# Moving the gate's rows and most second-layer weights to GpSimd's queue, the gate ahead of the weights, and query rows behind the contexts

## The chip, the cores and the metric

The kernel runs on one core of a Trainium2 chip. The metric is device time in microseconds (us), lower is better; a time is the median of several executions. The engines are named as in the profile: PE (TensorE matmul), PEld (its weight load), DVE (VectorE), ACT (ScalarE), POOL (GpSimd) and SP (SyncE). SP and POOL here do almost nothing but issue DMA transfers, each in the order of its own instruction stream.

## The reference

Two branches read the same input `x` (2048 rows of 512) and are mixed row by row with a gate. Branch A is attention with 32 query heads of 16 dimensions over one shared key and value head; branch B is a two-layer network with a squared ReLU. All is float32.

```
g = sigmoid((x * gate_w).sum(-1))                 # one number a row
q, k, v = x @ wq, x @ wk, x @ wv                  # 32 heads of 16; one head of 16; one of 16
a = softmax(q k^T / 4) v, heads joined, @ wo
h = relu(x @ w1 + b1) ** 2                        # 512 -> 1792
b = h @ w2 + b2                                   # 1792 -> 512
out = g * a + (1 - g) * b
```

## The kernel before, in words

The whole program is unrolled and its order is written out by hand: a Python planner follows modelled times of PE, DVE and ACT (`at_pe`, `at_dve`, `at_act`) and puts each instruction where its engine should be free. Waits are then added for every dependency, so an engine stands still where the model was too early.

**Attention.** The 2048 query rows are four chunks `c` of 512; each chunk has eight groups of four heads, so there are 32 groups `it`. A group is cut into 32 units of work `u`: 16 key tiles of 128, times two halves `q` of 256 rows. For each unit PE writes the scores (line 881), ACT (or DVE's copy at line 902, then ACT) makes the exponentials (line 918), and PE adds the context into an accumulator (line 938). `phase` writes scores for a block of 6 to 9 units, mixed with matmuls of another "unit" of dense work (a span), then `context` writes the contexts of the block. Scores run `AHEAD = 4` units before the contexts. Where a half is finished, `finish` (line 974) lets ACT copy the accumulator into a tile `accs`, of which there is one, and after the second half SP issues two transfers out of it: `oc` (line 999) and `lq` (line 1000).

**Query rows.** A dense unit of the query stage (`q_unit`, 15 of them in the loop, each a span) makes 128 query columns for one chunk, splits them in a high and a low part, and writes both to DRAM with `q_write`: `qs<-qr` from SP and `qs<-ql` from POOL (line 372); after each fourth one `qnorm` writes norms (`qs<-nrm`, line 436). `q_load` (line 445) fetches the rows of one group from there into one of two `qa` tiles, with eight SP transfers (line 450), each of which waits until the scores of the group before last are done.

**Gate.** `gates()` queues chores for DVE: `gate_load(i)` fetches two rows of tiles of `x` (512 KB) into one of two buffers, `stage` and `rows` (line 662), the first time also the gate's weights `gwb` (line 660); `gate_sum(i)` (line 670) multiplies and sums one of 16 tiles. A load goes out after the sums that used its buffer; its sums are held in the plan for `3 * LANDS` = 18 us. `gate_exps` and `gate` finish `g` and `1 - g`.

**Weights of the dense network.** `w_load(half)` fetches tile `n` of the first (`half` 0) or second (`half` 1) layer, 256 KB each, 14 a layer, into a staging place (`wf`, or half of a stage buffer; tile `n` uses the place of tile `n - 2`), by SP at line 491. `w_round` rounds it (ACT line 535 or DVE line 519) once `w_ready` says that more than `2 * LANDS` = 12 us of modelled PE time have gone by since the load; `w_rest` (line 528) takes the remainder, and asks for the next load, which is written at the end of the span. `w_keep` stores the split tiles to DRAM from POOL (line 514) for the later chunks. `room = [3, 4]` bounds how many split tiles there may be before the dense network begins, which is after the query stage.

**Order of DVE's extra work.** `soon` is a list of (span, cost, call): an entry is called at the latest at the start of that span, and earlier if DVE has time. `spend` fills DVE's gaps: first remainders of weights, then `soon`, divisions, roundings, biases, and then `chores` in their order, each with its modelled cost.

## Time and profile before

| | |
|---|---|
| median of 3 runs | 1183.03 us (1180.05 to 1184.37) |
| the profiled execution | 1185.62 us, of which the span from first to last instruction is 1183.7 us |
| PE, PEld, DVE, ACT, POOL busy | 1170.7, 783.6, 687.5, 1023.1, 72.1 us |
| DMA on SP's queue (q1) and on POOL's (q0) | 90.40 MB and 37.45 MB |

Rows of a timeline give start, duration, engine, line, operation, output and inputs, and in brackets the idle time of the engine just before and what ended it. The query stage, with the gate and the first weights beside it, takes about the first 150 us of the span; the rest is attention with the dense network and the output projection in between.

### The profile page before, as it was taken

What the parts mean: (1) busy time and instruction counts of PE and PEld (TensorE: products, weight loads), DVE (VectorE), ACT (ScalarE), POOL (GpSimd) and SP (SyncE); (2) the same over time, 40 slices, a digit from 0 to 9 for tenths busy, and PEclk for the clock granted to TensorE, in tenths of its full rate; (3) what the DMA queues carried; (4) which work ended last, traced back from release to release, by engine and by line L of the source; (5) the groups of instructions that cost most, each with busy time, mean ns of one, the idle gap of its engine ahead of it and who ended that gap; (6) DMA issues with size and microseconds to landing.
All of it is one profiled execution on the core that took longest, in us unless ns stands there. A gap on an engine that the chain in (4) does not pass through costs nothing.

```text
span 1183.7 us, 32009 instructions
## 1 busy us (share of the span) xinstructions
PE 1170.7 (99%) x13807; PEld 783.6 (66%) x13807; DVE 687.5 (58%) x1154; ACT 1023.1 (86%) x1133; POOL 72.1 (6%) x129
## 2 busy tenths in 40 slices
PE   9998999999999999999999999999999999999997
PEld 4665666676666666666666666666666666666664
DVE  6885777774764744463566636535556537544554
ACT  7796889998988888888888888888889889888884
POOL 1010101010100000100000000000000000001000
PEclk9998999999999999999999999999999999999999
DMA  7456444342253423230333404324214224322101
GB/s 255 128 155 170 116 145 171 101 161 105 98 178 119 163 71 104 96 99 29 117 135 113 136 6 143 128 65 153 64 47 154 90 65 131 109 72 79 56 37 38
DMA packets 53735, 130.25 MB, mean 110 GB/s; under 512 B 14218, under 2 KB 14714, under 8 KB 53080
## 3 DMA queue, kind: packets, MB, share of 16 engines
q1 hardware_dynamic: 38568, 90.40, 24.2%
q0 software_dynamic: 14736, 37.45, 9.6%
q8 instruction: 109, 1.79, 0.6%
q10 hardware_dynamic: 288, 0.33, 0.1%
q14 instruction: 34, 0.28, 0.1%
HBM read 87.91 MB, written 35.64 MB: 104 GB/s over the span
## 4 chain that ended last, share of the span: by engine, by line
PE 96%; DMA 2%; SPq 1%; ACT 1%; DVE 1%; issue 0%; DVEq 0%; ACTq 0%
PE acc L938 38%; PE mm L1245 32%; PE s L881 18%; PE x L881 5%; DMA stage<-in_xs 1%; SPq L450 1%; DMA oc<-accs 1%; ACT e L918 0%; PE acc L571 0%; PE mm L211 0%; PE mm L313 0%; DVE e L902 0%; DVE ot L1205 0%; PE s L322 0%; PE acc L358 0%
## 5 line engine op out<-in xcount | busy, mean ns | idle before, releaser
L918 ACT ACTIVATE e<-s 128x1024 f32<-128x1024 f32 x765 | 748.6, 1024 | 109.4 <-PE s L881 106.6
L902 DVE COPY e<-x 128x512 f32<-128x512 f32 x518 | 358.3, 692 | 450.5 <-PE x L881 295.2
L938 PE MATMUL acc<-e,v_ext 128*32 128x256 f32 x8192 | 470.2, 381 | 0.0
L881 PE MATMUL s<-qa,k_aug 49*128 49x512 f32 x1530 | 408.2, 411 | 1.4 <-ACT e L918 1.3
L938 PEld LDWEIGHTS acc<-e,v_ext 128*32 128x32 f32 x8192 | 252.3, 110 | 193.3 <-issue 40.8
L918 ACT ACTIVATE e<-e 128x1024 f32<-128x1024 f32 x259 | 272.9, 1056 | 0.9 <-DVE e L902 0.9
L881 PEld LDWEIGHTS s<-qa,k_aug 49*128 49x128 f32 x1530 | 214.6, 185 | 86.9 <-ACT e L918 41.3
L1245 PE MATMUL mm<-w2p,hr 64*128 64x512 f32 x1128 | 242.5, 392 | 0.0
L881 PE MATMUL x<-qa,k_aug 49*128 49x512 f32 x518 | 214.5, 414 | 3.7 <-DVE e L902 3.7
L1245 PEld LDWEIGHTS mm<-w2p,hr 64*128 64x128 f32 x1128 | 160.5, 186 | 18.5
L881 PEld LDWEIGHTS x<-qa,k_aug 49*128 49x128 f32 x518 | 95.5, 184 | 39.5 <-DVE e L902 21.7
L1245 PE MATMUL mm<-xragain,w1p 64*128 64x512 f32 x448 | 119.5, 392 | 0.0
L1245 PE MATMUL mm<-xr,w1p 64*128 64x512 f32 x448 | 114.9, 392 | 0.0
L1245 PEld LDWEIGHTS mm<-xragain,w1p 64*128 64x128 f32 x448 | 70.0, 186 | 6.4
L1245 PEld LDWEIGHTS mm<-xr,w1p 64*128 64x128 f32 x448 | 68.4, 186 | 6.0
L1245 PE MATMUL mm<-xlagain,w1p 64*128 64x512 f32 x224 | 69.5, 395 | 0.0
L1245 PE MATMUL mm<-xl,w1p 64*128 64x512 f32 x224 | 66.5, 393 | 0.0
L1245 PE MATMUL mm<-more 64*128 64x512 f32 x216 | 60.2, 393 | 0.0
L992 ACT ACTIVATE accs<-acc 128x256 f32<-128x256 f32 x60 | 23.1, 385 | 29.6 <-PE acc L938 25.8
L764 DVE TENSOR_SCALAR big<-mm,b1t 128x512 f32<-128x512 f32 x56 | 41.6, 742 | 0.0
L765 DVE TENSOR_TENSOR big<-big 128x512 f32<-128x512 f32 x56 | 38.8, 692 | 1.9
L1245 PEld LDWEIGHTS mm<-xlagain,w1p 64*128 64x128 f32 x224 | 35.6, 186 | 4.7
(188 smaller groups left out, 824.4 us busy)
## 6 DMA issues: line engine op xcount, KB each, us to landing
w1p<-w1kept SPq DMA_DIRECT2D x42, 512.0 KB
w2p<-w2kept SPq DMA_DIRECT2D x35, 512.0 KB
qa<-qs SPq DMA_DIRECT2D x186, 64.0 KB
w1kept<-w1p POOLq DMA_DIRECT2D x14, 512.0 KB, 4.2
w2kept<-w2p POOLq DMA_DIRECT2D x12, 512.0 KB, 5.6
qs<-qr SPq DMA_DIRECT2D x16, 256.0 KB
ress<-res POOLq DMA_DIRECT2D x4, 1024.0 KB, 4.6
qs<-ql POOLq DMA_DIRECT2D x15, 256.0 KB, 7.5
```

What stands on the lines that cost most here:

```text
L450: nc.sync.dma_start(q[64 * r + row:64 * r + row + b - a].bitcast(F32), qs[it, r, a:b])
L764: nc.vector.tensor_scalar(h[0], p, b1t[:, f:f + 1], 0.0, op0=OP.add, op1=OP.max)
L765: nc.vector.tensor_tensor(h[0], h[0], h[0], OP.mult)
L881: nc.tensor.matmul(dst.rearrange("p (a n) -> p a n", a=2), k_aug[rows, kt * 128:(kt + 1) * 128], qa[it][rows, :, q * HC:q * HC + HC], star ...
L902: nc.vector.tensor_copy(e_half(u)[:, 2 * r:2 * r + 2], x.rearrange("p (a n) -> p a n", a=2))
L918: nc.scalar.activation(e_half(u), src, AF.Exp, scale=SCALE)
L938: nc.tensor.matmul(accs[q][h * 32:(h + 1) * 32], v_ext[:, kt], es[u][:, h % 2 * 2 + h // 2], start=kt == 0 and it > 0, stop=kt == NK - 1, ...
L992: nc.scalar.activation(a[:, q * HC:q * HC + HC], acc, AF.Copy)
L1245: nc.tensor.matmul((self.before if r else self).bank, a[p], b[p], start=not r and i == 0, stop=r == 1 and i == len(self.terms[1]) - 1, ski ...
```

## The change

Four edits go together. `w_load` issues tiles 0 to 11 of both layers from POOL instead of SP, tiles 12 and 13 stay on SP. `gate_load` issues the gate's weights and rows from POOL. The first two pairs of weight loads leave `soon` and become chores behind the gate sums 8 and 10, and `gates()` is called at span 3 at the latest, not 5, with no loads ahead of it. In the main loop `context` comes ahead of `q_load`, so that the copies and transfers of finished sums are written before the query loads of that block. The bias rows `b2t`, 256 KB once, go from POOL to SP.

```diff
-                nc.sync.dma_start(wf[half][n], w12[n, :, half * 512:half * 512 + 512])
+                (nc.gpsimd if n < NF - 2 else nc.sync).dma_start(wf[half][n], w12[n, :, half * 512:half * 512 + 512])
...
-                (2, 0.0, lambda: (w_load(0), w_load(1))), (2, 0.7, lambda: (act(0.64), wq_round(0), wq_rest(0)))]
-        soon += [(5, 0.0, lambda: (w_load(0), w_load(1), gates()))]
+                (2, 0.7, lambda: (act(0.64), wq_round(0), wq_rest(0))), (3, 0.0, lambda: gates())]
...
-                nc.sync.dma_start(gwb, bass.AP(tensor=gw.tensor, offset=gw.offset, ap=[[0, 128], [1, D]]))
+                nc.gpsimd.dma_start(gwb, bass.AP(tensor=gw.tensor, offset=gw.offset, ap=[[0, 128], [1, D]]))
             if i < NS:
-                nc.sync.dma_start(gate_rows[i // 2 % 2], xs[i:i + 2].rearrange("t p d -> p t d"))
+                nc.gpsimd.dma_start(gate_rows[i // 2 % 2], xs[i:i + 2].rearrange("t p d -> p t d"))
...
+        def w_loads():
+            w_load(0)
+            w_load(1)
 
         def gates():
             chores.append((0.0, lambda: gate_load(0)))
...
                 chores.append((0.77, lambda i=i: gate_sum(i)))
+                if i in (NS - 8, NS - 6):
+                    chores.append((0.0, w_loads))
...
-                    nc.gpsimd.dma_start(b2t[0], bass.AP(tensor=b2.tensor, offset=b2.offset, ap=[[0, 128], [1, D]]))
+                    nc.sync.dma_start(b2t[0], bass.AP(tensor=b2.tensor, offset=b2.offset, ap=[[0, 128], [1, D]]))
...
             phase(slots, min(u + m + AHEAD, total) - scored, m)
+            context(range(u, u + m))
             it = (u + m - 1) // (2 * NK)
             if it not in begun_q and it + 1 < NC * NG:
                 begun_q.add(it)
                 q_load(it + 1)
-            context(range(u, u + m))
```

## The prediction

> **What bounds the kernel now.** I read the page first: is one engine the bound? Then the waits of that engine, then its timeline around each wait, and from there backwards to what came late.

> ```profile
> span 1183.7 us, 32009 instructions
> PE 1170.7 (99%) x13807; PEld 783.6 (66%) x13807; DVE 687.5 (58%) x1154; ACT 1023.1 (86%) x1133; POOL 72.1 (6%) x129
> ```

> TensorE (PE) is busy 99% of the span, so only time in which PE stands still, or runs slowly, can be won without removing matmuls, and this change removes none. The waits of PE, longest first (total, times, longest):

> ```profile
> PE x L881 <- DVE e L902: 3.7, 2, 3.4
> PE s L881 <- ACT e L918: 1.3, 1, 1.3
> ```

> Two waits matter, both in the query stage. To price them with what follows them I use the distance between the starts of successive context blocks (line 938) in PE's timeline:

> ```profile
> 85.72 2.80 PE L938 MATMUL acc<-e,v_ext 128*32 128x256 f32 x48
> 92.15 0.50 PE L881 MATMUL s<-qa,k_aug 49*128 49x512 f32 x2 [1.33 <-ACT e L918]
> 94.70 3.23 PE L938 MATMUL acc<-e,v_ext 128*32 128x256 f32 x56
> 102.48 3.23 PE L938 MATMUL acc<-e,v_ext 128*32 128x256 f32 x56
> 110.74 0.79 PE L881 MATMUL x<-qa,k_aug 49*128 49x512 f32 x1 [3.43 <-DVE e L902]
> 116.59 3.23 PE L938 MATMUL acc<-e,v_ext 128*32 128x256 f32 x56
> ...
> 124.38 2.80 PE L938 MATMUL acc<-e,v_ext 128*32 128x256 f32 x48
> 131.71 3.23 PE L938 MATMUL acc<-e,v_ext 128*32 128x256 f32 x56
> 139.47 3.23 PE L938 MATMUL acc<-e,v_ext 128*32 128x256 f32 x56
> ```

> Undisturbed, a block of 48 to the next takes 131.71 - 124.38 = 7.33 us, a block of 56 takes 139.47 - 131.71 = 7.76. The first wait's block took 94.70 - 85.72 = 8.98, that is 1.65 too long; the second's 116.59 - 102.48 = 14.11, that is 6.35 too long. The second costs nearly twice its 3.43 us of standstill, and the stretches of 4 us show why (the last three figures are the granted clock, the DMA share and GB/s):

> ```profile
> 108.00:112.00 4.00, 1.26 (x6) 1.07 (x8) 2.34 (x6) 0.35 (x1) 0.00 (x0) 0.71 0.69 211
> 112.00:116.00 4.00, 4.00 (x20) 3.10 (x20) 1.56 (x4) 2.06 (x3) 0.70 (x1) 0.50 0.39 131
> 116.00:120.00 4.00, 4.00 (x66) 1.87 (x62) 2.58 (x4) 2.90 (x3) 0.00 (x0) 0.93 0.48 81
> ```

> After the standstill the clock was granted at 0.50 until about 116.5. The shorter wait left it at full speed. Together 8.00 us are to be had here.

> What came late in each case stands in the rows of ACT and DVE, and in the chain of waits (start, length, piece):

> ```profile
> 90.80 0.38 ACT L992 ACTIVATE accs<-acc 128x256 f32<-128x256 f32 x1 [2.41 <-DMA oc<-accs]
> 109.38 0.69 DVE L670 SCALAR_TENSOR_TENSOR stage<-stage,gwb 128x512 f32<-128x512 f32 x1 [4.24 <-DMA stage<-in_xs]
> 84.12 6.60 DMA oc<-accs
> 93.78 15.57 DMA stage<-in_xs
> ```

> ACT may not overwrite the sums' tile until the transfer of the previous ones, issued at 84.12, has read it. DVE stands in a gate sum whose rows were issued at 93.78 and landed 15.57 us later. Both transfers were issued late, as SyncE's timeline shows (start, time from the first issue to the end of the last, issues):

> ```profile
> 75.84 8.19 SPq L450 DMA_DIRECT2D qa<-qs  x8
> 84.12 0.55 SPq L999 DMA_DIRECT2D oc<-accs  x1
> 86.42 4.49 SPq L491 DMA_DIRECT2D stage<-in_w  x2
> 91.01 2.67 SPq L436 DMA_DIRECT2D qs<-nrm  x4
> 93.78 0.78 SPq L662 DMA_DIRECT2D stage<-in_xs  x1
> 98.76 8.05 SPq L491 DMA_DIRECT2D wf<-in_w  x2
> ```

> The sums' transfer stood behind eight query loads (8.19 us). The gate's rows stood behind those, two weight loads (4.49) and four norm writes (2.67).

> **The change, part by part.**

> *Query rows behind the contexts.* The call that copies the finished sums issues `oc` and `lq` (lines 999, 1000) and now comes ahead of `q_load`. In the block of 75.84 the sums' transfer moves up by the 8.19 us of the query loads, to about 76, and with the same 6.60 us it has landed by 83, against ACT's need at 90.80 - 2.41 = 88.4. The 1.65 us go. The price: 31 sets of query loads now wait for the ACT copy and two issues. The next set is scored at the earliest 32 units after the copied ones, less the 4 units ahead and a block of 9: 19 units, and at 7.76/7 = 1.11 us each that is 21 us. The longest set of issues is

> ```profile
> 464.40 8.35 SPq L450 DMA_DIRECT2D qa<-qs  x8
> ```

> so 8.35 and about 1.1 for `oc` and `lq` leave 11 us for landing. I cost it at nothing; the cover is the 21 us of contexts, and if it were gone PE would wait in the scores of a head group, up to the missing part, at each of 31 boundaries.

> *Gate's rows on GpSimd, ahead of the weights.* Nine transfers (eight pairs of rows, `gwb`) leave SP for POOL. They are free of SP's order, but stand in POOL's, behind the writes of the low query parts:

> ```profile
> 79.34 0.69 DVE L411 TENSOR_TENSOR ql<-mm,qr 128x512 fp32r<-128x512 f32 x1
> 82.55 0.68 DVE L670 SCALAR_TENSOR_TENSOR stage<-stage,gwb 128x512 f32<-128x512 f32 x1
> ...
> 96.10 0.69 DVE L411 TENSOR_TENSOR ql<-mm,qr 128x512 fp32r<-128x512 f32 x1
> ...
> 84.09 0.72 POOL L372 DMA_DIRECT2D qs<-ql  x1 [6.66 <-DVE stage L670]
> 92.81 0.70 POOL L372 DMA_DIRECT2D qs<-ql  x1 [8.00 <-issue]
> 106.84 0.72 POOL L372 DMA_DIRECT2D qs<-ql  x1 [12.75 <-issue]
> ```

> The buffer for the late pair (rows 8 and 9) comes free with the sum at 82.55, at 83.23. POOL would then issue it at once behind the write of 84.09, at 84.8 instead of 93.78, 9 us sooner. Landing is bounded by the 512 KB write that POOL issued at 76.85 and by the 15.57 us of SP's:

> ```profile
> w1kept<-w1p POOLq DMA_DIRECT2D x1, 512.0 KB, 8.4
> qs<-ql POOLq DMA_DIRECT2D x1, 256.0 KB, 8.4
> qs<-ql POOLq DMA_DIRECT2D x1, 256.0 KB, 13.7
> ```

> So it lands between 93.2 and 100.4, and DVE wants it at 109.38 - 4.24 = 105.1: at least 4.7 us to spare. I take the low end, as the row of the same queue, size and stage. The 6.35 us go. Later pairs have the 18 us (three times LANDS) that the program allows from load to sum, less POOL's delay.

> That delay needs care. The write of 84.09 had its data at 80.03 and waited 4.1 us; that of 106.84 had it at 96.79 and waited 10.0. Each write went out when the one before it had landed: 84.09 + 8.4 is 92.5, and the next starts at 92.81; 92.81 + 13.7 is 106.5, and the next starts at 106.84. So POOL, 6% busy, is in this stage a chain of writes with loads behind it, and a load there is late by 0 to 10 us before it begins.

> *Weights.* The first four loads leave the start of the stage for a place behind gate sums 8 and 10; 24 loads (12 tiles, two layers: the edit applies to both) go to POOL, the last four stay on SP. Their first rounding comes at least 12 us (twice LANDS) after the load is written into the program. From the rows, delay and landing together are 4.1 + 8.4 = 12.5 at the low end and 10.0 + 9.1 = 19.1 at the high one (the 9.1 is that of

> ```profile
> w1kept<-w1p POOLq DMA_DIRECT2D x1, 512.0 KB, 9.1
> ```

> issued at 69.19). The shortfall is thus 0.5 to 7.1 us for a rounding at its earliest moment, and nothing for one that waits for the end of the next span but one (2 x 7.76 = 15.5). The only such wait in this stage so far is

> ```profile
> 98.12 0.63 ACT L535 ACTIVATE w2p<-stage 128x512 fp32r<-128x512 f32 x1 [0.48 <-DMA stage<-in_w]
> ```

> I take two roundings that come 1 us short; 2.41 us of idle ACT became 1.33 us of idle PE above, so this is 2 x 0.55 = 1.1 us. Bounds: 0 (all hidden) and 6.35 (one as bad as the gate's). It cannot be a gain, since the list of PE's waits holds nothing else between the start and the end of the span. DVE and ACT do as many roundings as before, later: three first-layer tiles must be ready from

> ```profile
> 142.97 0.39 PE L1245 MATMUL mm<-xr,w1p 64*128 64x512 f32 x1
> ```

> on (135 without the 8 us), one more each 7.76 us. With loads from about 98 and two spans a tile the first is rounded at about 114, the third at about 137, for use at 151. That is enough.

> *Issue work.* 33 issues at about 0.7 us go to a POOL that is 94% idle; one (`b2t`) goes to SP, for a use 20 us later. Nothing.

> **Sum.** -1.65 - 6.35 + 1.1 = -6.9 us. The profiled execution took 1185.62 us, 1.92 more than its span and 2.59 more than the median of the three runs; 1183.03 - 6.9 = 1176.1.

> [...]

> **The rivals.**

> 1. *The stall moves.* A later gate pair or a rounding comes late by as much as the gate's pair does now, 4.24 us on DVE, and PE's clock falls again. For it: POOL's 10.0 us of delay, and loads that bunch behind gate sums 8 and 10. Against: 18 us are allowed for a pair. Time: 1183.03 - 8.00 + 6.35 = 1181.4.
> 2. *It doesn't do what it says.* The transfer is as slow from POOL and the pair stays late; only the sums' wait goes. For it: the 13.7 us landing at 92.81, in the same crowd. Against: that crowd holds weight loads and writes that now come later. Time: 1183.03 - 1.65 = 1181.4.
> 3. *Slower.* The weights are the chain: each load stands behind a query write that stands behind the last one's landing, so that roundings between 110 and 140 wait in span after span. One costs 6.35; it decides from a shortfall of about 4 us on, that is a load that takes over 16 us from program to landing (the high end above is 19.1). Three of the six spans there: 1183.03 - 8.00 + 19.05 = 1194.1. Against: roundings are mostly written in at span ends, 15.5 us after.

> **How the numbers follow.** My forecast has 0.60, rival 1 has 0.22 (its ends overlap the weights' bounds), rival 2 has 0.08, rival 3 has 0.10. The forecast's own range is 1174 to 1178.5. About 0.5% (5.9 us, 1177.1) is what a measurement of this kernel can tell from no change, the three runs lying within 4.3 us; 0.53 of the forecast's 0.60 is below it. The rest of it and rivals 1 and 2 are no change: 0.37. Slower is rival 3: 0.10. The range for 8 in 10 runs from 1173.5 (all 8.00, and a run at the fast side) to 1182.5 (rivals 1 and 2 with a margin); it leaves out rival 3 and the far ends.

> **What would show it.** The gate ends with this row:

> ```profile
> 151.84 0.17 DVE L564 TENSOR_SCALAR g<-g 128x16 f32<-128x16 f32 x1
> ```

> Right: PE's waits hold neither the 3.4 nor the 1.3 us; the granted clock stays at 1.00 from 100 to 130; `oc` is issued ahead of `qa` in each group on SP; the gate is finished before 140 instead of 152; first-layer products start near 135. Wrong: a DVE or ACT row with idle time ended by a DMA of `stage`, `rows` or `wf` between 95 and 140; query loads that PE waits for; POOL's writes starting over 10 us behind their data.

## The result, and the profile after

The kernel after takes 1185.20 us in the median of 22 runs (1181.07 to 1194.44), the kernel before 1181.29 in 22 runs beside it (1177.29 to 1187.13): a ratio of 1.0045 with a 95% interval of 1.0027 to 1.0062. The forecast was 1176.1 and a gain; it became a loss of about 4 us. The profiled execution took 1188.94 us, 3.7 above that median.

The page of the kernel after first, span and busy time:

```profile
span 1187.2 us, 32000 instructions
PE 1171.1 (99%) x13807; PEld 784.5 (66%) x13807; DVE 687.8 (58%) x1154; ACT 1022.8 (86%) x1133; POOL 90.7 (8%) x161
```

PE is still the bound. Its waits in the kernel after (total, times, longest):

```profile
PE x L886 <- DVE e L907: 3.5, 1, 3.5
PE s L886 <- ACT e L923: 3.5, 1, 3.5
```

The names are those of before (881, 902 and 918 are now 886, 907 and 923, and the contexts' line 938 is 943), but they are two other stalls. Those of before are gone, as these rows of SP and then of DVE in the kernel after show:

```profile
74.06 0.55 SPq L1004 DMA_DIRECT2D oc<-accs  x1
...
75.63 3.99 SPq L450 DMA_DIRECT2D qa<-qs  x6
```

```profile
95.85 0.68 DVE L669 SCALAR_TENSOR_TENSOR stage<-stage,gwb 128x512 f32<-128x512 f32 x1
...
122.67 0.43 DVE L519 CAST w2p<-stage 128x512 fp32r<-128x512 f32 x1 [4.11 <-DMA stage<-in_w]
```

The sums' transfer `oc` goes ahead of the query loads, and the gate sums of rows 8 and 9 run without a wait, the first at 95.85; before, that one stood 4.24 us for its rows and ran at 109.38. The last row is a new wait, DVE's rounding of a weight. The second new one is on ACT:

```profile
168.13 0.63 ACT L535 ACTIVATE w1p<-wf 128x512 fp32r<-128x512 f32 x1 [4.29 <-DMA wf<-in_w]
```

What they cost is read from the starts of PE's context blocks around them, as in the prediction:

```profile
116.50 2.80 PE L943 MATMUL acc<-e,v_ext 128*32 128x256 f32 x48
...
130.20 3.32 PE L943 MATMUL acc<-e,v_ext 128*32 128x256 f32 x56
...
161.01 3.23 PE L943 MATMUL acc<-e,v_ext 128*32 128x256 f32 x56
...
173.42 3.89 PE L943 MATMUL acc<-e,v_ext 128*32 128x256 f32 x56
181.86 3.23 PE L943 MATMUL acc<-e,v_ext 128*32 128x256 f32 x56
```

The first took 13.70 us for a block of 48 that takes 7.33 undisturbed: 6.37 too long. The second took 12.41 and 8.44 for two blocks of 56 that take 7.76 each: 4.65 + 0.68 = 5.33 too long. Together 11.7 us, against 8.0 in the profiled execution of before; the spans differ by 3.5 (1187.2 - 1183.7). Each standstill, of 3.46 us, costs more than itself: as before, the granted clock is low for a while after it, read in steps of 1 us 0.50 from 124 to 130 and from 172 to 174 (here windows of 4 us of the kernel after, two around the first standstill and one after the second; the third figure from the end is the granted clock):

```profile
120.00:124.00 4.00, 0.90 (x8) 0.40 (x4) 1.33 (x4) 2.00 (x3) 1.11 (x2) 0.95 0.70 205
124.00:128.00 4.00, 3.64 (x18) 2.85 (x20) 2.41 (x5) 1.47 (x2) 0.00 (x0) 0.50 0.66 209
...
172.00:176.00 4.00, 4.00 (x44) 2.05 (x44) 2.98 (x5) 3.50 (x4) 1.09 (x2) 0.65 0.49 169
```

Why the loads were late is read in POOL's timeline of the kernel after:

```profile
75.77 0.74 POOL L661 DMA_DIRECT2D stage<-in_xs  x1 [1.03 <-DVE stage L669]
...
100.35 0.69 POOL L372 DMA_DIRECT2D qs<-ql  x1 [7.26 <-issue]
101.03 1.16 POOL L491 DMA_DIRECT2D wf<-in_w  x2
108.14 0.72 POOL L661 DMA_DIRECT2D stage<-in_xs  x1 [5.96 <-issue]
109.61 0.75 POOL L372 DMA_DIRECT2D qs<-ql  x1 [0.74 <-DVE e L907]
110.36 0.56 POOL L491 DMA_DIRECT2D stage<-in_w  x1
116.02 0.56 POOL L491 DMA_DIRECT2D stage<-in_w  x1 [5.10 <-issue]
...
146.83 0.65 POOL L968 DMA_DIRECT2D lc<-ls  x1 [7.05 <-DMA ls<-n]
147.53 0.72 POOL L372 DMA_DIRECT2D qs<-ql  x1
...
157.85 0.73 POOL L372 DMA_DIRECT2D qs<-ql  x1 [9.04 <-DVE e L907]
158.58 1.11 POOL L491 DMA_DIRECT2D wf<-in_w  x2
```

and in the landing times of this kernel's DMAs, first a row of the DMA view of 108.0 to 109.3 and one of that of 147.5 to 147.6, then two pieces of the chain of waits:

```profile
stage<-in_xs POOLq DMA_DIRECT2D x1, 512.0 KB, 7.6
...
qs<-ql POOLq DMA_DIRECT2D x1, 256.0 KB, 10.0
```

```profile
116.02 6.62 DMA stage<-in_w
...
158.58 9.47 DMA wf<-in_w
```

The first row of POOL's is the gate's pair that was late before, 18 us sooner. The two weight loads that DVE and ACT want at about 118 are written as a pair, but the second went out 5.66 us behind the first: at 116.02, 0.3 us after the gate pair issued at 108.14 had landed (108.14 + 7.6 = 115.7). In the second place the load stands behind two query writes and the fetch `lc`, which itself waited 7.05 us for `ls`. The second of these writes had its data from DVE at 148.0 and left at 157.85, again 0.3 us after the landing of the one before (147.53 + 10.0 = 157.5); the row names DVE as what ended the idle time, but the landing fits the moment.

### The profile page after: what moved, and what is told of

It reads as the page before. It is cut to its first block, busy times and chain, and to the rows that moved or that the text cites. A ratio compares the mean times of both kernels' runs of the same rounds, so it can differ in the third digit from the quotient of the medians.

```text
span 1187.2 us, 32000 instructions
## 1 busy us (share of the span) xinstructions
PE 1171.1 (99%) x13807; PEld 784.5 (66%) x13807; DVE 687.8 (58%) x1154; ACT 1022.8 (86%) x1133; POOL 90.7 (8%) x161
## 4 chain that ended last, share of the span: by engine, by line
PE 95%; DMA 2%; issue 1%; DVE 1%; ACT 1%; POOL 0%; SPq 0%; POOLq 0%; DVEq 0%; ACTq 0%
PE acc L943 38%; PE mm L1250 32%; PE s L886 18%; PE x L886 5%; DMA wf<-in_w 1%; DMA stage<-in_w 1%; ACT e L923 0%; DMA xf<-in_xT 0%; PE mm L211 0%; DVE e L907 0%; DVE ot L1210 0%; PE mm L313 0%; PE s L322 0%; PE acc L358 0%; PE s L211 0%
## 5 line engine op out<-in xcount | busy, mean ns | idle before, releaser
L923 ACT ACTIVATE e<-s 128x1024 f32<-128x1024 f32 x765 | 747.9, 1024 | 108.1 <-PE s L886 105.3
## 6 DMA issues: line engine op xcount, KB each, us to landing
w1p<-w1kept SPq DMA_DIRECT2D x42, 512.0 KB
w2p<-w2kept SPq DMA_DIRECT2D x35, 512.0 KB
w1kept<-w1p POOLq DMA_DIRECT2D x14, 512.0 KB, 4.0
w2kept<-w2p POOLq DMA_DIRECT2D x12, 512.0 KB, 5.1
qs<-qr SPq DMA_DIRECT2D x16, 256.0 KB
qs<-ql POOLq DMA_DIRECT2D x15, 256.0 KB, 7.9
```

Source lines behind the costliest of these rows:

```text
L923: nc.scalar.activation(e_half(u), src, AF.Exp, scale=SCALE)
```

## The experiments

### One part alone

**e1**, only the contexts ahead of the query loads, in the kernel before:

```diff
+            context(range(u, u + m))
             it = (u + m - 1) // (2 * NK)
...
-            context(range(u, u + m))
```

> The kernel before with one edit: contexts ahead of the query loads; gate and weights as before. Both theories: oc goes out at about 74 instead of 84, the 1.3 us wait of PE for ACT goes, the block that took 8.98 us takes 7.3, the gate's wait of 3.4 us with the clock at half stays. Time 1.65 us less than before (ratio 0.9986). If query loads behind the copies cost anything, PE's scores wait at head groups and the ratio is above 1.

Measured: 1177.69 (eleven of 12 runs 1177.14 to 1179.45, one 1183.83), ratio 0.9983 [0.9965, 1.0001]. SP's timeline in e1:

```profile
74.96 0.54 SPq L999 DMA_DIRECT2D oc<-accs  x1
...
92.54 0.39 SPq L662 DMA_DIRECT2D stage<-in_xs  x1
```

The sums' wait went, as in the prediction. So did the gate's, which was not expected: its pair went out at 92.54 instead of 93.78, its sum ran at 103.77 without a wait, and PE's longest wait in the query stage was 0.3 us. The 1.24 us do not suffice for that: the pair must also have landed in under 11.3 us (103.77 - 92.54), against 15.57 before. The gate's stall of before thus hung on little, and the cheapest part of the change removed both.

**e5**, only the weights on POOL, in the kernel before (early as there):

```diff
-                nc.sync.dma_start(wf[half][n], ...)
+                (nc.gpsimd if n < NF - 2 else nc.sync).dma_start(wf[half][n], ...)
```

> The kernel before with one edit: weight tiles 0 to 11 are loaded from GpSimd; order, gate and query loads as before. Theory A (GpSimd's queue holds loads back behind the query writes): the loads written in at about 72 and 86 go out some 4 to 8 us later than they did from SP, DVE or ACT waits 2 to 4 us for a weight between 85 and 110, and the time is 0 to 0.5% above before (ratio 1.000 to 1.005), though the gate's rows come sooner from SP. Theory C (what hurts is that the weights begin 70 us later, the queue matters little): no wait at a rounding, the gate's wait is gone, ratio 0.996 to 0.999.

Measured: 1181.74 (1177.87 to 1189.39), ratio 1.0012 [0.9990, 1.0034]. The ratio is inside theory A's range, but the waits that A forecast are not there: the profiled run had no rounding that waited over 0.2 us, and lost its time elsewhere (a low clock at the start, 0.993 in the mean of the run; see the end). In that run the queue alone doesn't make the loss: loads that are early enough stand it. The other runs above 1181 were not profiled.

**e11**, the gate on POOL and the contexts ahead, in the kernel before, the weights left on SP and early:

```diff
-                nc.sync.dma_start(gwb, ...)
+                nc.gpsimd.dma_start(gwb, ...)
...
-                nc.sync.dma_start(gate_rows[i // 2 % 2], ...)
+                nc.gpsimd.dma_start(gate_rows[i // 2 % 2], ...)
...
+            context(range(u, u + m))
...
-            context(range(u, u + m))
```

> The kernel before with contexts ahead of the query rows and the gate's rows on POOL, the weights as before (on SP, early): the change without its weights. Theory A: the gate pairs can each be held by a query write's landing, but 18 us cover it: no wait of PE over 1 us, median 1177 to 1179.5, ratio 0.996 to 0.999. Rival C (the gate's pairs on POOL are themselves what stalls): 1181 to 1185, ratio 1.000 to 1.004.

Measured: 1178.34 (ten of 12 runs 1176.91 to 1179.48), ratio 0.9988 [0.9970, 1.0006]; PE's longest wait at scores is 0.8 us, as theory A said. The gate's move and the contexts' show no harm; the loss is in the weights' part.

### The weights: queue, order, margin

**e2**, the kernel after with all weights back on SP, still behind gate sums 8 and 10:

```diff
-                (nc.gpsimd if n < NF - 2 else nc.sync).dma_start(wf[half][n], ...)
+                nc.sync.dma_start(wf[half][n], ...)
```

> The changed kernel with all weight loads on SP again; gate on GpSimd, ahead of the weights, contexts ahead. Theory A (the late roundings come from GpSimd's queue, which holds a load back until earlier writes have landed): the waits of 4.1 us (DVE, near 122) and 4.3 us (ACT, near 168) are under 1 us, and the kernel is 7 to 8 us faster than before (ratio 0.993 to 0.995). Theory B (any queue is too slow for loads that are rounded 12 us after they are written in, in this crowd): waits of 3 us or more stay at the roundings, ratio 1.00 to 1.005.

Measured: 1179.47, in two heaps (six runs 1177.08 to 1177.52, six 1181.42 to 1185.22), ratio 1.0001 [0.9979, 1.0022]. The profiled run, 1183.12, is of the upper heap and has no wait at a rounding over 0.6 us; its loss is the low clock at the start again. So the waits went, as theory A said, but not its gain of 0.5% or more. In four runs of the upper heap, the profiled one among them, the mean granted clock is 0.993 or 0.994; in the other two (1182.50 and 1185.22) it is 0.997, as in the profiled run of e9, which has a stall; what they lost is open.

**e10**, the kernel after with the weights and the gate on SP, so that the order alone is new:

```diff
-                (nc.gpsimd if n < NF - 2 else nc.sync).dma_start(wf[half][n], ...)
+                nc.sync.dma_start(wf[half][n], ...)
...
-                nc.gpsimd.dma_start(gwb, ...)
+                nc.sync.dma_start(gwb, ...)
...
-                nc.gpsimd.dma_start(gate_rows[i // 2 % 2], ...)
+                nc.sync.dma_start(gate_rows[i // 2 % 2], ...)
```

> The kernel after with gate and weights all on SP: only the order (gate ahead of the weights, contexts ahead of the query rows) is changed against the kernel before. Theory A (the queue makes the loss): no wait of PE over 1 us, median 1177 to 1179.5, ratio 0.996 to 0.999. Rival B (the later place of the weights makes it): a rounding waits for its load, PE stands still for 2 to 4 us, 1183 to 1186, ratio 1.001 to 1.005.

Measured: 1178.66, ratio 0.9992 [0.9976, 1.0007]; nine of 12 runs 1177.00 to 1179.11, three 1181.64 to 1183.56. By the median theory A holds. But the profiled run (span 1181.7) is one of those three, and it has the first stall of the kernel after, at the same rounding; PE stands still for 4.4 us. Its SP and DVE timelines:

```profile
105.79 9.43 SPq L450 DMA_DIRECT2D qa<-qs  x8
115.27 0.94 SPq L491 DMA_DIRECT2D stage<-in_w  x2
```

```profile
123.33 0.50 DVE L519 CAST w2p<-stage 128x512 fp32r<-128x512 f32 x1 [4.96 <-DMA stage<-in_w]
```

Here the pair stood behind eight query loads on SP and went out at 115.27; in the kernel after half of it stood behind the gate pair on POOL until 116.02. So rival B is right for this run: the new order leaves the load so little time, 12 modelled us to its rounding, that a delay in either queue makes it late. On SP most runs show no loss by their times; with the kernel after's queue no run of 22 came below 1181.

**e9**, the kernel after with the gate on SP, the weights late and on POOL. Theory A in its first form wanted the gate's 512 KB pairs in the crowd:

```diff
-                nc.gpsimd.dma_start(gwb, ...)
+                nc.sync.dma_start(gwb, ...)
...
-                nc.gpsimd.dma_start(gate_rows[i // 2 % 2], ...)
+                nc.sync.dma_start(gate_rows[i // 2 % 2], ...)
```

> The kernel after with the gate's rows and weights back on SP (the first twelve tiles of both layers still on POOL, still behind gate sums 8 and 10). Theory A (POOL's queue is held by the landing of what went before, and the gate's 512 KB pairs are part of that): without the pairs the weight loads wait for one query write at most, the roundings' waits shrink to under 1 us on PE, median 1178 to 1181.5, ratio 0.997 to 1.000. Rival B (weights that are late by the order alone, or by the query writes alone, on POOL): stalls of 3.5 us at one or two roundings as in the kernel after, median 1184 to 1186, ratio 1.003 to 1.006.

Measured: 1187.35 in 6 runs (1184.82 to 1189.74), ratio 1.0057 [1.0035, 1.0080]: A's form with the gate pairs fell and rival B's ratio came, with a median 1.35 us above B's range. The first stall is gone (both halves of the pair left together at 106.73), the second is there. POOL and then ACT in e9:

```profile
142.58 0.64 POOL L968 DMA_DIRECT2D lc<-ls  x1 [6.95 <-DMA ls<-n]
143.29 0.96 POOL L372 DMA_DIRECT2D qs<-ql  x1
...
153.65 0.73 POOL L372 DMA_DIRECT2D qs<-ql  x1 [8.83 <-issue]
154.53 1.12 POOL L491 DMA_DIRECT2D wf<-in_w  x2
```

```profile
162.87 0.63 ACT L535 ACTIVATE w1p<-wf 128x512 fp32r<-128x512 f32 x1 [5.57 <-DMA wf<-in_w]
```

So in the kernel after it is the gate pair that makes the first stall. The second doesn't need it: there the load stands behind the query writes and `lc`.

**e4**, the kernel after with 18 instead of 12 modelled us between load and rounding:

```diff
-                    and at_pe - since[half][n] > 2 * LANDS)
+                    and at_pe - since[half][n] > 3 * LANDS)
```

> The changed kernel with the modelled time from a weight load to its rounding raised from 12 to 18 us (three times LANDS), nothing else. Both theories: the loads are as late as in the changed kernel, but roundings come a span later; the two waits (4.1 and 4.3 us) go, ratio 0.993 to 0.996. If the weights then run short at the start of the dense network, DVE rounds in a hurry near 140 to 180 and PE waits there for 2 us or more: ratio about 1.00.

Measured: 1185.76 (1181.37 to 1192.81), ratio 1.0054 [1.0029, 1.0079]. This is worse than either expectation. In the profiled run (span 1180.4) the two stalls are gone, but the products of the dense network wait for roundings that now come late. PE's waits in e4:

```profile
PE mm L1250 <- DVE w2p L519: 1.1, 2, 0.6
PE mm L1250 <- DVE w1p L528: 0.9, 4, 0.2
```

These six waits sum to 2.0 us. The span of e4 is 5.4 us longer than that of e3 (below, 1175.0). So the larger margin moves the shortage from the rounding to its use, as far as this one trace shows; how 2.0 us of waits become 5.4, and why three of the 12 runs took over 1192, is open. The kernel after itself has no such wait, so the prediction's "That is enough" held there.

### The reserve

**e3** and **e6**, the kernel after with 1280 and with 768 bytes reserved instead of 1024; **e7**, the kernel before with 1280:

```diff
-    nc = bacc.Bacc(..., dynamic_dma_scratch_size=1024)
+    nc = bacc.Bacc(..., dynamic_dma_scratch_size=1280)
```

> The changed kernel with the program's reserve for GpSimd's descriptors raised from 1024 to 1280 bytes, nothing else. Theory A with the reserve as its cause: a query write no longer waits for the landing of the one before, the second load of the pair goes out within 1 us of the first instead of 5.7 us later, both waits at roundings shrink under 1 us, ratio 0.993 to 0.996. If the delay is not a matter of the reserve (theory B, or a dependency between the writes): the writes still start 0.3 us after the landing of the one before, ratio about 1.004. [...]

> The changed kernel with the reserve for GpSimd's descriptors lowered from 1024 to 768 bytes, nothing else. Theory A with the reserve as its cause: fewer loads fit behind a query write, gate pairs wait for landings too, roundings are later by some 5 us more, ratio to before 1.008 to 1.015. If the reserve is not the cause: as the changed kernel, 1.0045. [...]

> The kernel before with the reserve raised from 1024 to 1280 bytes, nothing else: does the larger reserve help by itself? Theory A: POOL's query writes go out as soon as their data is there, but no compute engine waits for them; the sums' wait and the gate's wait on SP stay, ratio 0.999 to 1.001. If the larger reserve itself were the gain of the run with 1280 bytes, 0.997.

| | median us | ratio to before |
|---|---|---|
| after, 768 | 1227.22 | 1.0412 [1.0396, 1.0428] |
| after, 1024 | 1185.20 | 1.0045 [1.0027, 1.0062] |
| after, 1280 (e3) | 1177.08 | 0.9972 [0.9951, 0.9993] |
| before, 1280 (e7) | 1177.67 | 0.9985 [0.9974, 0.9997] |

POOL's timeline in e3:

```profile
92.39 0.72 POOL L372 DMA_DIRECT2D qs<-ql  x1 [6.18 <-DVE e L907]
96.07 0.69 POOL L372 DMA_DIRECT2D qs<-ql  x1 [2.96 <-DVE ql L411]
96.75 0.58 POOL L491 DMA_DIRECT2D wf<-in_w  x1
99.76 0.56 POOL L491 DMA_DIRECT2D wf<-in_w  x1 [2.43 <-issue]
...
105.31 0.76 POOL L372 DMA_DIRECT2D qs<-ql  x1 [4.25 <-DVE rows L669]
106.06 1.10 POOL L491 DMA_DIRECT2D stage<-in_w  x2
```

The second write leaves 3.68 us after the first; the two take 8.0 us to landing in the median, so by that the first is still under way. What ended POOL's wait is now DVE's `ql`, the data; in the kernel after the write left 5.0 us after its data. The queue can still hold a load back: the second `wf` load left at 99.76, after 2.43 us of idle time for which the profile names no releaser. But the pair that was late leaves whole at 106.06, and PE's waits hold nothing between the start and the end of the span. The ratio, 0.9972, is a gain, though less than the 0.993 to 0.996 expected. With 768 bytes, PE's waits (e6):

```profile
PE x L886 <- DVE e L907: 14.6, 4, 6.3
PE s L886 <- ACT e L923: 10.2, 3, 5.1
PE x L886 <- DVE tmp L365: 10.0, 1, 10.0
```

The loss, 4.1%, is far above the 0.8 to 1.5% expected. Nothing differs in these kernels but the reserve, so theory A holds as far as this: the reserve decides (1.0412, 1.0045 and 0.9972 at 768, 1024 and 1280 bytes). The rows say the same of single transfers: in the kernel after, the query write of 100.35 left 0.4 us after that of 92.36 had landed (7.6 us, so 99.96), in e3 that of 96.07 left 3.68 us after that of 92.39. They also show behind what a load waited: in the kernel after a gate pair, a write and one load (108.14 to 110.36), in e3 two writes and one load (92.39 to 96.75). How much of the reserve a transfer takes no run counts.

e7 helped by itself, a little more than A expected, and against A both waits of before are gone from its trace. The query loads are still ahead of `oc` on SP, but SP's queue ran ahead (`oc` at 82.86 instead of 84.12, the gate pair at 90.18 instead of 93.78), and all 12 runs lay between 1176.73 and 1178.20. That the writes which leave when their data is ready make SP's queue faster is not shown.

**e12**, e9 with 1280 bytes, to see whether the reserve or the place in the order makes the second stall:

```diff
-    nc = bacc.Bacc(..., dynamic_dma_scratch_size=1024)
+    nc = bacc.Bacc(..., dynamic_dma_scratch_size=1280)
```

> The kernel of e9 (the gate on SP, the weights late and on POOL) with 1280 instead of 1024 bytes reserved for POOL's descriptors. Theory A' (what holds POOL's queue is the room for descriptors, with or without the gate's pairs): query writes leave when their data is ready, the load that e9 issued at 154.53 and had at 162.87 goes out some microseconds earlier, no rounding waits over 1 us, median 1177 to 1179, ratio 0.996 to 0.999. Rival B (the place behind the write of ls, for which the fetch of lc waits 7 us, and behind the query writes in the program's order): room doesn't help, the same rounding waits 3 to 6 us, median 1183 to 1188, ratio 1.003 to 1.007.

Measured: 1178.33 (1177.46 to 1179.55), ratio 0.9984 [0.9969, 0.9999]; the longest wait at the rounding is 1.1 us, and PE's there 0.3. The time is as A' said, one step of it isn't: the load did not go out earlier (154.73, against 154.53 in e9). It was still held: POOL stood idle for 4.83 us ahead of it, and the profile names no releaser. POOL's timeline and the chain of waits show what did change (both of e12):

```profile
149.17 0.73 POOL L372 DMA_DIRECT2D qs<-ql  x1 [4.68 <-DVE hr L203]
154.73 1.11 POOL L491 DMA_DIRECT2D wf<-in_w  x2 [4.83 <-issue]
```

```profile
154.73 3.63 DMA wf<-in_w
```

The write ahead of the load left 4.5 us sooner (149.17, not 153.65), that is 5.56 us ahead of the load instead of 0.88, and the load took 3.6 us instead of 8.25. In e9 that write took 6.9 us to landing; if it took as long in e12, an estimate, most of it was over when the load began. That the transfers' sharing makes this difference is argued from the two traces, not tried by itself.

**e8**, contexts ahead and 1280 bytes in the kernel before, meant to beat both:

```diff
+            context(range(u, u + m))
...
-            context(range(u, u + m))
...
-    nc = bacc.Bacc(..., dynamic_dma_scratch_size=1024)
+    nc = bacc.Bacc(..., dynamic_dma_scratch_size=1280)
```

> A version meant to beat both kernels: the kernel before with contexts ahead of the query loads (all loads on SP, the weights first) and the reserve at 1280 bytes. Theory A: as contexts ahead alone, no wait of PE over 0.5 us between 40 and 1170, median near 1177.5, ratio 0.997 to 0.999.

Measured: 1177.65 (twelve runs 1177.04 to 1177.94, two 1183.11 and 1183.48), ratio 0.9983 [0.9973, 0.9993]. Its median and ratio beat both kernels, as e7's and e3's do, but no more than those of e1 or e7 alone: each of these traces is free of the stalls of before. The profiled run of e8 is one of the two above 1183, by the low clock at the start (mean 0.994).

## Why the prediction was wrong

- **Contexts ahead of the query loads: right.** `oc` goes at 74.06, the 1.65 us went, and no score waits for query rows, in e1 or in the kernel after.
- **The gate on POOL: right in the mechanism.** The late pair went out at 75.77, its sums ran at 95.85, the 6.35 us went; the gate ended at 145.24, not 151.84. That is later than the "before 140" of the prediction, and the first-layer products began at 141.60, not near 135; both are put off by the first new stall: without its 6.37 us they would, as an estimate, stand at 138.87 and 135.23.
- **The weights: the step that failed, a term of the sum that was mis-sized.** It stood at 1.1 us, two roundings 1 us short. Two came short by 4.1 and 4.3 us, inside the 0.5 to 7.1 us that the prediction worked out for a rounding at its earliest moment, and cost 6.37 + 5.33 = 11.7 us in the profiled execution. What talked the bound down was the sentence that roundings are mostly written in at span ends, 15.5 us after the load. The first late one wasn't: POOL began its pair at 110.36, and DVE stood ready for it at 122.67 - 4.11 = 118.6, 8.2 us later; the second began at 158.58, and ACT stood ready at 168.13 - 4.29 = 163.8, 5.3 us later. In e3, with 1280 bytes, the first pair left at 106.06. The bound of 6.35 us was also for one rounding, and there were two. What came lies between two rivals: the first stall is rival 1's in size, with the load held by the gate pair's landing, and the second is rival 3's chain of query writes.
- **The stall that went was not all there to be won.** The sum took 8.00 us, the stalls of one execution, off the median 1183.03. But before's runs reach from 1177.3 to 1187.1, and e1, e3, e7 and e8, whose traces have none of these stalls, have most of their runs at 1176.7 to 1178: that is the floor. The median of before's 22 runs lies about 4 us above it, so 1183.03 - 8.00 = 1175.0, before the weights' 1.1, asked for more than there was. Its own execution, 1185.62 - 8.00 = 1177.6, gives the floor rightly, and so does that of the kernel after, 1188.94 - 11.7 = 1177.2; the subtraction from another run's time was the error. From 1177.2 the median of after, 1185.20, is 8.0 us, so by this estimate the miss of 9.1 us is 2.2 of floor and 6.9 of weights (8.0 - 1.1). The best version (e3) gained 0.28%, below the 0.5% that the chances called a gain.
- **Landings ahead of a load: read in the rows of before, priced too low.** The prediction quotes query writes that leave 0.3 us after the landing of the one before, and has a load behind them late by 0 to 10 us. The gate's pair of rows 12 and 13 did wait for a landing: it left at 108.14, 0.3 us after the write of 100.35 had landed (7.5 us, so 107.85). But it had 18 us, and what ran out was the weights' 12. What the rows mean for small loads in the same queue was priced from both ends, and a value near the low end taken.

So: the order leaves the weights too little time (e10), POOL's queue makes them late (the traces of after and e9; by their times all 22 and 6 runs, none of which came below 1181), and a reserve of 1280 bytes takes the stalls away (e3, e12). Not settled is how often the order alone makes the stall, and what two runs in the upper heap of e2 lost.

## What to carry to other kernels

An engine that is 8% busy, as POOL is in the kernel after, can still hold loads back: look at what ends the waits of its DMA rows, and if a write leaves just behind the landing of the last one (0.3 us here), try a larger reserve, which took the ratio here from 1.0045 to 0.9972. A load put into this queue waited for the landing of the gate pair ahead of it and went out 5.66 us behind the other load of its pair. When a load's start is moved, compare its worst path (delay plus landing) with the margin the program gives its first use, and price the far end if the profile shows it once. Take a stall off the execution that shows it, and compare the result with the lowest times of the kernel before: a forecast below these may have counted on time that was not there.

## What the runs showed that had not been expected

- **The clock at the start.** In the profiled runs of e2, e5 and e8 the granted clock falls early (0.993, 0.993 and 0.994 in the mean of the run), which by the spans costs about 6 us: 1181.2, 1182.5 and 1181.7, against 1175.0 to 1176.7 in e1, e3, e7, e11 and e12, at 0.999 to 1.000. The first windows of it in e2:

```profile
20.00:24.00 4.00, 3.52 (x29) 2.63 (x28) 3.87 (x9) 2.31 (x5) 0.00 (x0) 1.00 0.29 66
24.00:28.00 4.00, 4.00 (x16) 3.36 (x16) 2.84 (x6) 2.75 (x3) 0.00 (x0) 0.60 0.26 101
28.00:32.00 4.00, 4.00 (x23) 3.25 (x22) 1.36 (x3) 3.51 (x4) 1.14 (x2) 0.50 0.01 6
```

  In the next two windows the clock is 0.50 and 0.70; from 24 to 40 that is a mean of 0.575, as much as 13.6 us at 0.50 and the rest at 1.00. In e5 and e8 single matmuls of the query projection take 0.63 us near 25.3, where e3 has 0.39. PE stood still for only 0.5 us ahead of it in e2, for a split weight of the query projection. The profiled runs of e2, e5 and e8 share that wait (0.5, 0.9 and 0.5 us), and no other profiled run has it; why so short a one is followed by so long a stretch of low clock was not tried. Runs near 1183 with a mean clock of 0.993 to 0.995, in versions that are otherwise near 1177 (e1, e3, e8, e11), look the same, but most were not profiled.
- **Standstills and the clock.** After the 1.33 us in before the clock stayed at 1.00 (88 to 96). After the 3.43 us in before and both of 3.46 us in the kernel after it was granted at 0.50, read in steps of 1 us. In e9 and e10, after 4.76 and 4.38 us, the window of 4 us in which PE begins again has 0.65 and 0.69. Length alone does not decide it: at the start of e2, e5 and e8 the clock fell after a standstill of 0.9 us at most. What does decide it is not shown.
- **256 bytes of reserve** decided more than the four edits together: with them the same program has 0.9972 instead of 1.0045, and the kernel before, without the edits, 0.9985.
